# Attention and MLP on one core: dividing the eight PSUM banks 3 + 2 + 3 instead of 3 + 3 + 2

## The chip, the cores and the metric

The kernel runs on one core of a Trainium2 chip. Time is microseconds of device time for one execution. Three runs of the kernel before gave a median of 809.33 us (809.15 to 810.74). Besides these there is one execution taken by the profiler, from which every row and duration of the text comes.

## The reference

Two transformer layers over one sequence of 2048 rows of width 448, with the same weights in both. Each layer adds attention and then an MLP to its input:

```python
x = x + A(layernorm(x))      # A: softmax(q k^T * 28**-0.5) v, 16 heads of 28, then @ wo
x = x + B(layernorm(x))      # B: relu(h @ w1 + b1)**2 @ w2 + b2, 448 -> 1792 -> 448
x = x + A(layernorm(x))
x = x + B(layernorm(x))
```

Softmax needs one exponential for each of 2 x 16 x 2048 x 2048 scores. This is what fills the kernel's time.

## The kernel before, in words

**Units.** The scores are cut into 2048 units of 128 partitions x 512 columns of fp32, and one unit fills one PSUM bank. A unit belongs to a head, a few key blocks and a block of queries. The scores of a unit are K times Q (line 1106, four heads side by side in the rows of the array), then the exponential turns them into bf16 in SBUF (tile pts), then P times V (line 1335, into a bank called oT) uses them. A pass is all units of one layer, query block and group of four heads. The reference's maximum is not subtracted before the exponential, and the sum for the softmax comes out of P times V by a column of ones in V.

**Two ways to an exponential.** ScalarE does most units: one ACTIVATE with Exp (line 1138) over a whole score group, 1536 columns for three units (called wide in the text) or 1024 for two (narrow). The others go to VectorE and GpSimd, which work it out with integer tricks: VectorE reads the scores out of PSUM (line 1210), GpSimd makes a correction of it (1235, 1250), and VectorE squares and adds (1241, 1262, 1274). Such a unit is called VectorE's.

**PSUM.** The eight banks are two score tiles of three banks each (pool ps_sc, resource R_sc) and two spare banks (pools ps_m, resources R_m). While ScalarE reads one score tile, TensorE fills the other. The spare banks hold everything else that TensorE makes: the tiles of projections and of the MLP (mt, line 834), transposes (tp), P times V (oT). At the very beginning, and once the last scores are sent, these may also use score tiles (pools_now).

**Where VectorE's scores lie.** s_stream sends the score groups one after the other. It takes the next three units. Then either a fourth unit goes to VectorE in a spare bank (the branch with OWN3, `own`), or the group is cut to two units and the third bank of its tile gets a unit for VectorE (the branch with THIRD): ScalarE then reads two banks, VectorE the third, and the tile is free when both have read. The order has 373 wide and 298 narrow exponentials, and 333 units for VectorE: 298 in third banks and 35 in spare ones.

**What sets the order.** Planner.run is a list scheduler that runs when the kernel is built. Streams (scores, exponentials, P times V, projections, layer norm, fillers for TensorE) offer their next operation; the planner keeps a clock for each engine, and takes what can start earliest, by priority. So every engine's queue is fixed when the kernel is built, and on the chip each engine works through its queue in that order, waiting on semaphores. Tables of 128 numbers, one for each 16 units, steer it: OWN3 (may a fourth unit go to a spare bank here), PACE (how much VectorE may have waiting before it gets another unit), MIXT (whether GpSimd makes the second part of a unit). `apart` decides whether VectorE gets a unit at all. To keep TensorE's clock up, the planner repeats score matmuls while there is room (`again`) and adds fillers (`heat`, line 1766).

**Opening and tail.** The first exponential needs layer norm, transposes and the first K and Q of the first rows; layer norm's blocks for later rows are transposed by DMA (line 716). After the last exponential come P times V of the last rows, the normalisation, the output projection, layer norm, and the last rows' MLP (finish, ends_last).

Of the kernel before, what the change touches and what calls it, by code (L numbers as in the profile page):

```python
# [75 lines left out]
PRE = 0.5  # L76
# [22 lines left out]
OWN3 = (0.0, 0.0, 0.0, 0.0, 0.0, 0.0, 1.0, 1.0, 0.0, 0.0, 0.0, 0.0, 1.0, 0.0, 1.0, 1.0, 1.0, 1.0, 0.0, 1.0, 0.0, 0.0, 1.0, 0.0, 1.0, 1.0, 1.0, 0.0, 0.0, 0.0, 0.0, 1.0, 1.0, 1.0, 0.0, 0.0, 0.0, 1.0, 0.0, 1.0, 1.0, 0.0, 1.0, 0.0, 0.0, 0.0, 0.0, 0.0, 0.0, 1.0, 0.0, 0.0, 0.0, 0.0, 1.0, 0.0, 0.0, 0.0, 0.0, 0.0, 1.0, 1.0, 0.0, 0.0, 0.0, 1.0, 1.0, 0.0, 0.0, 0.0, 1.0, 0.0, 0.0, 1.0, 1.0, 0.0, 0.0, 1.0, 0.0, 0.0, 0.0, 0.0, 0.0, 0.0, 0.0, 0.0, 0.0, 0.0, 1.0, 0.0, 0.0, 1.0, 0.0, 1.0, 1.0, 0.0, 1.0, 1.0, 1.0, 1.0, 0.0, 0.0, 0.0, 0.0, 1.0, 0.0, 1.0, 1.0, 0.0, 1.0, 0.0, 0.0, 0.0, 0.0, 1.0, 1.0, 1.0, 0.0, 0.0, 0.0, 0.0, 0.0, 0.0, 0.0, 0.0, 0.0, 0.0, 0.0)  # L99
# [9 lines left out]
LEAD = 15  # L109
LAST = 690  # L110
BUSY = 0.995
PACE = (1.4, 3.0, 3.0, 1.4, 3.0, 1.4, 2.2, 4.0, 3.0, 3.4, 3.0, 3.0, 4.0, 2.2, 3.0, 3.0, 3.0, 3.4, 3.4, 3.4, 2.2, 2.2, 3.4, 3.0, 3.4, 4.0, 2.2, 3.0, 4.0, 3.0, 3.0, 4.0, 4.0, 3.4, 3.4, 4.0, 4.0, 3.4, 3.0, 4.0, 3.0, 4.0, 3.0, 4.0, 3.0, 3.0, 2.2, 3.0, 3.0, 3.4, 3.0, 3.0, 3.0, 3.0, 3.4, 4.0, 3.4, 4.0, 2.2, 4.0, 4.0, 4.0, 3.0, 2.2, 2.2, 2.2, 3.0, 3.0, 3.0, 3.0, 4.0, 4.0, 2.2, 4.0, 3.0, 4.0, 3.0, 3.4, 4.0, 3.0, 3.0, 1.4, 3.0, 3.4, 3.0, 4.0, 1.4, 3.4, 3.4, 4.0, 3.0, 2.2, 3.0, 3.0, 4.0, 3.4, 3.0, 4.0, 3.0, 2.2, 3.4, 2.2, 3.0, 3.4, 3.0, 4.0, 3.0, 3.0, 1.4, 4.0, 3.0, 3.0, 3.0, 2.2, 3.0, 2.2, 3.4, 3.0, 3.0, 3.0, 3.0, 3.0, 3.0, 3.0, 3.0, 3.0, 3.0, 3.0)
MIXT = (1.8, 1.2, 1.8, 1.2, 1.2, 1.8, -9.0, 1.2, 1.2, 1.8, 1.2, 1.2, 1.8, 1.2, 1.2, 1.8, 1.2, 1.2, -9.0, 1.2, 1.2, 1.2, 1.2, 1.2, -9.0, 1.8, 1.2, 1.2, 1.2, 1.2, -9.0, 1.2, 1.8, 1.2, 1.8, -9.0, 1.8, 1.2, 1.2, 1.2, 1.8, 1.2, 1.2, 1.2, 1.2, 1.2, 1.8, 1.2, 1.8, 1.2, 1.2, 1.2, 1.2, 1.2, -9.0, 1.8, 1.2, 1.8, 1.2, 1.2, 1.8, 1.2, -9.0, 1.2, -9.0, -9.0, 1.2, -9.0, 1.2, 1.8, 1.2, 1.8, -9.0, 1.2, 1.8, 1.8, 1.8, -9.0, 1.8, 1.2, 1.8, 1.2, 1.2, 1.8, 1.2, 1.2, 1.8, 1.2, 1.8, 1.8, -9.0, 1.2, -9.0, 1.8, 1.8, 1.2, 1.8, 1.2, 1.2, -9.0, -9.0, 1.2, 1.2, 1.2, 1.2, 1.2, -9.0, 1.2, -9.0, 1.2, 1.2, 1.2, -9.0, 1.2, -9.0, 1.2, 1.2, -9.0, 1.2, 1.2, 1.8, 1.8, 1.2, 1.2, 1.2, 1.2, 1.2, 1.2)
# [4 lines left out]
NPT = 12  # L118
# [4 lines left out]
LASTP = (3.2, 3.2, 3.2, 3.2, 3.2, 3.2, 3.2, 3.2, 3.2, 3.2, 3.2, 3.2, 3.2, 3.2, 3.2, 3.2, 3.2, 3.2, 3.2, 3.2, 3.2, 3.2, 3.2, 3.2, 3.2, 3.2, 3.2, 3.2, 3.2, 3.2, 3.2, 3.2, 3.2, 3.2, 3.2, 3.2, 3.2, 3.2, 3.2, 3.2, 3.2, 3.2, 3.2, 3.2, 3.2, 3.2, 3.2, 3.2, 3.2, 3.2, 3.2, 3.2, 3.2, 3.2, 3.2, 3.2, 3.2, 3.2, 3.2, 3.2, 3.2, 3.2, 3.2, 3.2, 3.2, 3.2, 3.2, 3.2, 3.2, 3.2, 3.2, 3.2, 3.2, 3.2, 3.2, 3.2, 3.2, 3.2, 3.2, 3.2, 3.2, 3.2, 3.2, 3.2, 3.2, 3.2, 3.2, 3.2, 3.2, 2.6, 3.2, 3.2, 3.2, 3.2, 3.2, 2.6, 1.5, 3.2, 2.6, 1.5, 3.2, 1.5, 3.2, 3.2, 3.2, 3.2, 1.5, 3.2, 4.4, 3.2, 3.2, 3.2, 3.2, 3.2, 3.2, 3.2, 3.2, 3.2, 3.2, 3.2, 3.2, 3.2, 3.2, 3.2, 3.2, 3.2, 3.2, 3.2)  # L123
# [15 lines left out]
LEND = 2  # L139
# [243 lines left out]
def kernel(  # L383
# [37 lines left out]
    ps_sc = ctx.enter_context(tc.tile_pool(name="ps_sc", bufs=2, space=bass.MemoryType.PSUM))  # L421
    ps_m = [ctx.enter_context(tc.tile_pool(name=f"ps_m{i}", bufs=1, space=bass.MemoryType.PSUM)) for i in range(2)]
# [4 lines left out]
    R_sc, R_m, R_pt = Res(2), (Res(1), Res(1)), Res(NPT)  # L427
# [612 lines left out]
    def s_stream():  # L1040
        while at[0] < len(units):
            gi = len(gbuf)
            js = ahead(3)
# [3 lines left out]
            def fn(e, gi=gi, us=us, js=js):  # L1047
                sc = ps_sc.tile([P, 3 * 512], DT.float32, name="sc", tag="sc")
# [10 lines left out]
                if OWN3[step[0]] > 0 and bank_free(o.start) and next_at(js[-1] + 1):  # L1059
# [7 lines left out]
                else:  # L1067
# [5 lines left out]
                    gbuf[gi]["in"] = not own and units[j][0] == us[0][0]  # L1073
# [25 lines left out]
                for i in list(range(4)) * (again + 1):  # L1099
                    for k, (pi, kb, r, hh) in enumerate(us):  # L1100
                        if i >= r:
# [9 lines left out]
                                   deps=list({d for u in us for d in needs(u)}), acq=R_sc, mode="row", sets=("s", gi))  # L1111
# [706 lines left out]
```

## Time and profile before

| | |
|---|---|
| median of three runs | 809.33 us |
| the profiled execution | 808.23 us, span 806.4 us |
| busy: ScalarE | 787.9 us (98%) |
| busy: VectorE | 765.0 us (95%) |
| busy: TensorE matmul | 758.2 us (94%) |
| busy: GpSimd | 483.4 us (60%) |
| first exponential begins | 10.71 us |
| last exponential ends | 792.9 us |
| granted TensorE clock | 1.000 |

PE is TensorE, PEld its weight loads, DVE VectorE, ACT ScalarE, POOL GpSimd; xN is a number of instructions. In a row of instruction groups stand the line, the engine, the operation, output<-inputs by the program's names with their shapes, and the count; then busy microseconds together and the mean nanoseconds of one; then idle time of the engine just before them, and what ended most of it. In a row of the timeline stand the start, the length of an unbroken run, and in brackets the idle time before it with what ended it; the run is listed under the shape of its first instruction. A row of waits reads "who <- for whom: us in total, times, longest". Neighbouring ScalarE instructions overlap in the records, so the sum of their durations is more than their busy time.

### The profile page before, as it was taken

The page shows a single profiled execution, that of the slowest core. Times are in us where ns is not written, and L with a number is a line of the kernel's source. Part 1 is how long each engine was busy: PE and PEld are TensorE (multiplying, and loading weights), DVE is VectorE, ACT ScalarE, POOL GpSimd, SP SyncE. Part 2 cuts the span into 40 slices and gives each one's busy share as a digit, 9 for nine tenths or more (in the row PEclk, how much of TensorE's full clock was granted, in tenths as well). Part 3 has the DMA queues.
Part 4 walks back from the last instruction along what each step waited for, and adds up shares of the span by engine and source line. Part 5 has one row for each costly group of instructions (what it writes and reads, how often), then busy time and mean ns, then how long its engine had stood idle before and what let it go on. Part 6 is the DMA issues. An engine that isn't in the chain of part 4 may idle for free.

```text
span 806.4 us, 27435 instructions
## 1 busy us (share of the span) xinstructions
PE 758.2 (94%) x11275; PEld 389.2 (48%) x11275; DVE 765.0 (95%) x1705; ACT 787.9 (98%) x686; POOL 483.4 (60%) x750
## 2 busy tenths in 40 slices
PE   8999989999899998999999998989899999999998
PEld 5544544444544544444544544434354444445565
DVE  7999999999999999999999998999999999999965
ACT  8999999999999999999999999999999999999994
POOL 3264656777676666866566666675665666666310
PEclk9999999999999999999999999999999999999999
DMA  9210010111002011001000000011100101010100
GB/s 249 84 22 9 15 23 10 22 22 22 19 4 35 10 22 21 5 20 22 15 16 15 13 3 15 9 21 25 34 21 14 34 14 34 10 26 9 31 16 13
DMA packets 59566, 20.66 MB, mean 26 GB/s; under 512 B 45289, under 2 KB 58987, under 8 KB 59440
## 3 DMA queue, kind: packets, MB, share of 16 engines
q1 hardware_dynamic: 59440, 18.91, 10.4%
q8 instruction: 88, 1.44, 0.8%
q14 instruction: 38, 0.31, 0.1%
HBM read 10.28 MB, written 1.95 MB: 15 GB/s over the span
## 4 chain that ended last, share of the span: by engine, by line
PE 39%; ACT 25%; DVE 24%; issue 9%; DMA 2%; POOL 1%; ACTq 0%; DVEq 0%; POOLq 0%
ACT pts L1138 25%; PE mt L834 19%; PE sc L1106 11%; PE oT L1335 7%; DVE v_w L1210 5%; DVE r L1531 3%; DVE pts L1262 2%; DMA xnT<-xn 2%; DVE pts L1241 2%; DVE st L661 2%; DVE K_sb L1210 1%; DVE x_sb L1473 1%; DVE V_sb L1241 1%; DVE V_sb L1540 1%; DVE V_sb L1262 1%
## 5 line engine op out<-in xcount | busy, mean ns | idle before, releaser
L1138 ACT ACTIVATE pts<-sc 128x1024 bf16<-128x1024 f32 (+1 forms) x671 | 777.8, 1321 | 5.0 <-PE sc L1106 4.2
L1106 PE MATMUL sc<-Q_sb,K_sb 32*128 32x256 bf16 (+1 forms) x4414 | 275.6, 265 | 31.2 <-ACT pts L1138 27.5
L1106 PEld LDWEIGHTS <-K_sb 32*128 32x128 bf16 x4484 | 102.8, 92 | 205.9 <-issue 145.6
L1250 POOL TENSOR_SCALAR v_w<-v_w 128x512 int16<-128x512 f32 x229 | 151.7, 662 | 65.9 <-DVE pts L1262 15.0
L1335 PE MATMUL oT<-pts,V_sb 128*32 128x256 bf16 (+1 forms) x4000 | 153.9, 268 | 0.8 <-DVE pts L1262 0.2
L1210 DVE TENSOR_SCALAR v_w<-sc 128x512 f32<-128x512 f32 x218 | 147.8, 681 | 2.9 <-PE sc L1106 2.1
L834 PE MATMUL mt<-xnT,w 128*128 128x256 bf16 (+1 forms) x888 | 119.4, 271 | 4.2 <-DVE r L1531 2.8
L1235 POOL TENSOR_SCALAR pts<-v_w 128x512 bf16<-128x512 uint16 x123 | 86.4, 703 | 53.2 <-DVE v_w L1210 15.6
L1335 PEld LDWEIGHTS <-V_sb 128*32 128x32 bf16 x4352 | 89.9, 96 | 51.2 <-issue 41.7
L1235 POOL TENSOR_SCALAR V_sb<-v_w 128x512 bf16<-128x512 uint16 x99 | 68.1, 688 | 47.5 <-DVE v_w L1210 11.5
L834 PEld LDWEIGHTS <-w 128*128 128x128 bf16 x896 | 75.2, 97 | 39.8 <-issue 30.6
L1250 POOL TENSOR_SCALAR K_sb<-K_sb 128x512 int16<-128x512 f32 x92 | 61.3, 666 | 32.2 <-DVE V_sb L1262 3.8
L1531 DVE TENSOR_SCALAR r<-mt 128x512 bf16<-128x512 f32 x108 | 73.8, 683 | 4.1 <-PE mt L834 1.9
L834 PE MATMUL mt<-w,V_sb 128*128 128x448 bf16 (+2 forms) x288 | 68.2, 346 | 0.0
L1241 DVE TENSOR_TENSOR pts<-pts 128x512 bf16<-128x512 bf16 (+1 forms) x124 | 64.7, 522 | 0.5 <-POOL pts L1235 0.5
L1210 DVE TENSOR_SCALAR K_sb<-sc 128x512 f32<-128x512 f32 x80 | 54.5, 682 | 5.5 <-PE sc L1106 4.7
L1241 DVE TENSOR_TENSOR V_sb<-V_sb 128x512 bf16<-128x512 bf16 (+1 forms) x106 | 56.4, 532 | 0.3 <-POOL V_sb L1235 0.3
L1262 DVE TENSOR_TENSOR pts<-pts,v_w 128x512 int16<-128x512 bf16 (+1 forms) x106 | 47.9, 452 | 0.9 <-POOL v_w L1250 0.5
L1473 DVE TENSOR_TENSOR x_sb<-x_sb,mt 128x448 bf16<-128x448 bf16 x61 | 37.2, 611 | 4.2 <-PE mt L834 3.9
L1235 POOL TENSOR_SCALAR V_sb<-K_sb 128x512 bf16<-128x512 uint16 x39 | 28.7, 736 | 20.6 <-DVE K_sb L1210 6.2
L1235 POOL TENSOR_SCALAR pts<-K_sb 128x512 bf16<-128x512 uint16 x43 | 29.6, 689 | 16.4 <-DVE V_sb L1262 3.5
L661 DVE BATCH_NORM_STATS2 st<-x_sb 128x6 f32<-128x448 bf16 x63 | 38.6, 615 | 0.9 <-DMA x_sb<-in_A_x_dram 0.7
(149 smaller groups left out, 854.1 us busy)
## 6 DMA issues: line engine op xcount, KB each, us to landing
rec<-scr SPq DMA_DIRECT2D x54, 64.0 KB
x_sb<-in_A_x_dram SPq DMA_DIRECT2D x8, 224.0 KB
out_dram<-x_sb SPq DMA_DIRECT2D x15, 112.0 KB
w<-in_B_w_dram SPq DMA_DIRECT2D x1, 1568.0 KB
w<-in_B_w_dram SPq DMA_DIRECT2D x1, 1344.0 KB
dn<-oT_sb SPq DMA_DIRECT2D x54, 2.0 KB
xnT<-xn SPq DMA_TRANSPOSE x50
V_sb<-in_A_wqkv_dram SPq DMA_DIRECT2D x4, 168.0 KB
```

The source lines that it names most:

```text
L661: return nc.vector.bn_stats(out=box["st"][:, :], in_=x_sb[:, t0 + j, :] if src is None else src())
L834: nc.tensor.matmul(box["t"][:, c0:c0 + n], lhsT=lhsT() if callable(lhsT) else lhsT, rhs=rhs, start=a, stop=b)
L1106: nc.tensor.matmul(dst[k][:, i * nt * P:(i + 1) * nt * P], lhsT=K_sb[l][rows, g, (kb + i) * P:(kb + i + 1) * P], rhs=Q_sb[rows, g, t0 * P: ...
L1138: t = nc.scalar.activation(out=pt[:, 0:n], in_=gbuf[gi]["sc"][:, 0:n], func=AF.Exp, scale=float(np.log(2.0)) * 2.0 ** -FRAC)
L1210: t = nc.vector.tensor_scalar(out=box["w"], in0=two(src), scalar1=EXP_SHIFT, scalar2=EXP_LOW, op0=ALU.add, op1=ALU.max)
L1235: return nc.gpsimd.tensor_scalar(out=two(pd), in0=low, scalar1=-EXP_MID * 65536, scalar2=EXP_BEND, op0=ALU.add, op1=ALU.mult)
L1241: return nc.vector.tensor_tensor(out=pd, in0=pd, in1=pd, op=ALU.mult)
L1250: return nc.gpsimd.tensor_scalar(out=two(box["t"]), in0=box["w"], scalar1=EXP_BITS, scalar2=1.0, op0=ALU.add, op1=ALU.mult)
L1262: return nc.vector.tensor_tensor(out=pd.bitcast(DT.int16), in0=pd, in1=t, op=ALU.add)
L1335: nc.tensor.matmul(box["t"][DHP * hh:DHP * hh + DHP, 0:n], lhsT=V_sb[l][:, kb + i, 4 * g + hh, :], rhs=p[:, c0:c0 + n], start=begin and kb ...
L1473: return nc.vector.tensor_tensor(out=x_sb[:, tb, lo:hi], in0=x_sb[:, tb, lo:hi], in1=t[:, 0:hi - lo], op=ALU.add)
L1531: return nc.vector.tensor_scalar(out=r[:, 0:w], in0=t[:, 0:w], scalar1=0.0, scalar2=None, op0=ALU.max)
```

## The change

- PSUM is divided anew: a score tile of three banks, one of two (`WIDE = (3, 2)`, pools ps_sc0 and ps_sc1), and three spare banks instead of two. The groups use the tiles in turn, so ScalarE reads three banks, two, three, two.
- VectorE's units no longer take the third bank of a group (`THIRD = 0`). They are all sent along with a group into a spare bank: with a narrow group wherever `apart` allows it, with a wide one where OWN3 allows it as well. What VectorE makes of a unit sent along with a narrow group may go into that group's free third of its pts slot (`gbuf[gi]["in"]`).
- Each score tile is a resource of its own: group gi waits for tile gi % 2, and nothing but ScalarE's exponential frees it.
- P times V and long matmul tiles that used to wait until both spare banks were free wait until two of the three are (`OPEN_M`).
- The tables OWN3 (107 ones, 44 before), PACE and MIXT are set anew; LASTP, STOPS and CPRE become constants, and LAST = 9999 no longer limits anything.

```diff
-LAST = 690
+LAST = 9999
...
-THIRD = 1
+THIRD = 0
+WIDE = (3, 2)
+OPEN_M = 2
+MMB = 3
+UNB = 0
...
-    ps_sc = ctx.enter_context(tc.tile_pool(name="ps_sc", bufs=2, space=bass.MemoryType.PSUM))
-    ps_m = [ctx.enter_context(tc.tile_pool(name=f"ps_m{i}", bufs=1, space=bass.MemoryType.PSUM)) for i in range(2)]
+    ps_sc = [ctx.enter_context(tc.tile_pool(name=f"ps_sc{i}", bufs=1, space=bass.MemoryType.PSUM)) for i in range(2)]
+    ps_m = [ctx.enter_context(tc.tile_pool(name=f"ps_m{i}", bufs=1, space=bass.MemoryType.PSUM)) for i in range(8 - sum(WIDE))]
...
-    R_sc, R_m, R_pt = Res(2), (Res(1), Res(1)), Res(NPT)
+    R_sc, R_m, R_pt = (Res(1), Res(1)), tuple(Res(1) for _ in ps_m), Res(NPT)
...
+    def scores(i):
+        return ps_sc[i].tile([P, WIDE[i] * 512], DT.float32, name="sc", tag="sc")
...
-                return R_m if all(r.when() is not None for r in R_m) else ()
+                return R_m[:MMB] if sum(r.when() is not None for r in R_m[:MMB]) >= OPEN_M else ()
...
-        if len(units) - i < STOPS[step[0]] or not LEAD <= len(gbuf) <= LAST:
+        if len(units) - i < STOP or not LEAD <= len(gbuf) <= LAST:
...
-            js = ahead(3)
+            js = ahead(WIDE[gi % 2])
...
-                sc = ps_sc.tile([P, 3 * 512], DT.float32, name="sc", tag="sc")
+                sc = scores(gi % 2)
...
-                if OWN3[step[0]] > 0 and bank_free(o.start) and next_at(js[-1] + 1):
+                if (OWN3[step[0]] > 0 or len(us) < 3) and bank_free(o.start) and next_at(js[-1] + 1):
                     j = apart(at[0], o.start, us)
                 elif len(us) == 3 and THIRD:
...
-                    gbuf[gi]["in"] = not own and units[j][0] == us[0][0]
+                    gbuf[gi]["in"] = len(us) < 4 and units[j][0] == us[0][0]
...
-                                   deps=list({d for u in us for d in needs(u)}), acq=R_sc, mode="row", sets=("s", gi))
+                                   deps=list({d for u in us for d in needs(u)}), acq=R_sc[gi % 2], mode="row", sets=("s", gi))
```

The change adds lines, so line 1106 of before is 1112 now, 1138 is 1144, 834 is 840 and 1210 is 1216.

How it moves instructions is seen in the built order of each engine's queue. First ScalarE's queue from the first Q tile on; pts is the output of the exponential, sc a score tile, and "x14" means 14 such instructions in a row. Before:

```order
L851 ACTIVATE Q_sb<-sc 128x2x256
L1138 ACTIVATE pts<-sc 128x1536 x14
L1138 ACTIVATE pts<-sc 128x1024 x2
L1138 ACTIVATE pts<-sc 128x1536 x6
L1138 ACTIVATE pts<-sc 128x1024 x4
L1138 ACTIVATE pts<-sc 128x1536 x3
```

And the same place now, with the numbers of the tiles:

```order
L857 ACTIVATE Q_sb_107<-mt_232 128x2x256
L1144 ACTIVATE pts_119<-sc_266 128x1536
L1144 ACTIVATE pts_119<-sc_273 128x1024
L1144 ACTIVATE pts_119<-sc_294 128x1536
L1144 ACTIVATE pts_119<-sc_322 128x1024
L1144 ACTIVATE pts_119<-sc_331 128x1536
```

Wide and narrow ones now take turns from the first group to the last, also where VectorE takes no units; before, narrow ones stood only where VectorE had the third bank. Over the whole program there are 346 wide and 347 narrow ones now, 693 in place of 671, and 316 units for VectorE in place of 333, all of them in spare banks.

Second, TensorE's queue ahead of the first scores; xnT is the transposed layer norm of the first rows, wk and wq are weights, sc_254 and sc_266 are the first score tiles. Of several matmuls that read alike one is shown. Before:

```order
L834 MATMUL sc_226<-xnT_168,wq_90 128x256
L834 LDWEIGHTS wk_91
L834 MATMUL mt_239<-xnT_168,wk_91 128x256
L1106 LDWEIGHTS K_sb0_99
L1106 MATMUL sc_254<-Q_sb_101,K_sb0_99 128x256
```

And now:

```order
L840 MATMUL mt_232<-xnT_174,wq_96 128x256
L840 LDWEIGHTS wk_97
L840 MATMUL mt_244<-xnT_174,wk_97 128x256
L840 LDWEIGHTS wq_96
L840 MATMUL mt_260<-xnT_174,wq_96 128x256
L1112 LDWEIGHTS K_sb0_105
L1112 MATMUL sc_266<-Q_sb_107,K_sb0_105 128x256
```

Four matmuls of the second Q tile (mt_260), which stood behind the first two score groups, stand ahead of the first one now; the first Q tile (mt_232) lies in a spare bank where it lay in a score tile.

More of the change, by code (lines that the diff above doesn't have):

```diff
@@ L1078, in fn @@
                         x = gbuf[gi]["x"] = Op("PE", 0.0, None)
-                        x.res = min((r for r in R_m if r.when() is not None), key=lambda r: r.when())
+                        x.res = (lambda f: f[-1] if UNB else min(f, key=lambda r: r.when()))([r for r in R_m if r.when() is not None and (not UNB or r.when() <= o.start)])
                         x.turn = len(x.res.rel)
```

17 lines of the change are left out of this document (8 added, 9 removed).

## The prediction

> **What bounds the kernel now.** I read the page's busy times first, then the busy time by stretch, then ScalarE's own timeline, and last the two shapes of its exponential.
>
> ```profile
> PE 758.2 (94%) x11275; PEld 389.2 (48%) x11275; DVE 765.0 (95%) x1705; ACT 787.9 (98%) x686; POOL 483.4 (60%) x750
> core 0: us, PE busy (x) PEld busy (x) DVE busy (x) ACT busy (x) POOL busy (x), PEclk, DMA share, GB/s
> 0.00:10.70 10.70, 9.32 (x65) 5.49 (x65) 7.04 (x29) 7.68 (x10) 4.77 (x13) 1.00 0.79 211
> 10.70:792.90 782.20, 738.46 (x11091) 376.27 (x11088) 750.54 (x1651) 777.76 (x671) 478.05 (x736) 1.00 0.10 23
> 792.90:806.40 13.50, 10.39 (x124) 7.44 (x122) 7.46 (x26) 2.49 (x6) 0.56 (x1) 1.00 0.06 19
> ```
>
> Three engines look full, but only one is. Between 10.7 and 792.9 us ScalarE does nothing but its 671 exponentials, and is busy for 777.76 of 782.20 us; VectorE and TensorE have 32 and 44 us to spare there. So the time is an opening of 10.7 us, a chain of exponentials, and a tail of 13.5 us. ScalarE's timeline shows where that chain breaks:
>
> ```profile
> 10.71 6.82 ACT L1138 ACTIVATE pts<-sc 128x1536 bf16<-128x1536 f32 x5 [0.61 <-PE sc L1106]
> 18.00 81.82 ACT L1138 ACTIVATE pts<-sc 128x1536 bf16<-128x1536 f32 x70 [0.46 <-PE sc L1106]
> 100.06 40.93 ACT L1138 ACTIVATE pts<-sc 128x1536 bf16<-128x1536 f32 x34 [0.24 <-PE sc L1106]
> 141.24 89.23 ACT L1138 ACTIVATE pts<-sc 128x1024 bf16<-128x1024 f32 x78 [0.25 <-PE sc L1106]
> 230.75 57.49 ACT L1138 ACTIVATE pts<-sc 128x1536 bf16<-128x1536 f32 x50 [0.28 <-PE sc L1106]
> 288.49 33.19 ACT L1138 ACTIVATE pts<-sc 128x1536 bf16<-128x1536 f32 x29 [0.24 <-PE sc L1106]
> 322.27 1.02 ACT L1138 ACTIVATE pts<-sc 128x1024 bf16<-128x1024 f32 x1 [0.59 <-PE sc L1106]
> 323.45 156.53 ACT L1138 ACTIVATE pts<-sc 128x1536 bf16<-128x1536 f32 x136 [0.16 <-PE sc L1106]
> 480.19 18.35 ACT L1138 ACTIVATE pts<-sc 128x1536 bf16<-128x1536 f32 x16 [0.22 <-ACT pts L1138]
> 499.93 292.99 ACT L1138 ACTIVATE pts<-sc 128x1024 bf16<-128x1024 f32 x252 [1.38 <-PE sc L1106]
> ```
>
> A row is one unbroken run (the shape printed is that of its first instruction); the bracket is the idle time ahead of it. Inside the chain there are nine, 3.8 us together (what else is idle lies in gaps too short for a row of their own), each a score group that TensorE delivered late. Whatever the change does, it has to show in this chain, in its ends, or not at all.
>
> **The change part by part.**
>
> *ScalarE's work.* The price of one exponential comes from these rows: the two shapes, the first instruction alone, and a run of 21 wide ones.
>
> ```profile
> L1138 ACT ACTIVATE pts<-sc 128x1536 bf16<-128x1536 f32 x373 | 533.7, 1511 | 2.4 <-PE sc L1106 2.0 <-ACT pts L1138 0.2
> L1138 ACT ACTIVATE pts<-sc 128x1024 bf16<-128x1024 f32 x298 | 305.8, 1083 | 2.6 <-PE sc L1106 2.2
> 10.71 1.45 ACT L1138 ACTIVATE pts<-sc 128x1536 bf16<-128x1536 f32 x1 [0.61 <-PE sc L1106]
> 764.61 28.32 ACT L1138 ACTIVATE pts<-sc 128x1536 bf16<-128x1536 f32 x21
> ```
>
> Neighbours overlap, so the cost is the step from one to the next: (28.32 - 1.45) / 20 = 1.3435 us for a wide one. The mean durations differ by 1511 - 1083 = 428 ns, the price of one more bank, so a narrow one costs 0.9155 us, and 1.3435 - 3 x 0.428 = 0.06 us of each is fixed. Before: 373 x 1.3435 + 298 x 0.9155 = 773.9 us. So 782.2 - 773.9 = 8.3 us of the chain is lost: 4.4 us idle (782.20 - 777.76), and 3.9 us in instructions that began late and overlapped less.
>
> The order of the changed kernel has 346 wide and 347 narrow exponentials. 373 x 3 + 298 x 2 = 1715 units before, 346 x 3 + 347 x 2 = 1732 now; of 2048 units VectorE keeps 316 where it had 333. ScalarE gets 17 units x 0.428 = 7.3 us and 22 instructions x 0.06 = 1.3 us: **+8.6 us**, all on the path. The chain without any loss is then 782.6 us, as long as the chain of before with all its losses. That is the core of this forecast: the change can at best give back what it takes.
>
> [...]
>
> *The losses.* What can the change give back? Two gaps are TensorE standing in its queue before a transposed block that a DMA brings, with the next scores behind it:
>
> ```profile
> 320.81 1.03 PE L834 MATMUL mt<-xnT,wk 128*128 128x256 bf16 x8 [0.94 <-DMA xnT<-xn]
> 498.90 0.60 PE L834 MATMUL mt<-xnT,wk 128*128 128x256 bf16 x4 [1.45 <-DMA xnT<-xn]
> 139.89 0.92 PE L834 MATMUL mt<-wo,oTn 128*128 128x448 bf16 x4 [0.23 <-DVE oT_sb L1362]
> 287.50 0.36 PE L834 MATMUL mt<-w,K_sb 128*128 128x448 bf16 x1 [0.20 <-DVE K_sb L1210]
> PE sc L1106 <- ACT pts L1138: 27.5, 61, 0.9
> PEld L1106 <- DVE v_w L1210: 10.6, 35, 0.8
> ```
>
> They cost ScalarE 0.59 + 0.16 + 1.38 = 2.1 us, and a PSUM bank more doesn't make a DMA land sooner: they stay, perhaps at other places. The 0.46 us at 18.00, in the opening, stays too: 2.6 of the 4.4 us. The rest, 1.8 us, are gaps of a quarter of a microsecond behind rows like the one at 139.89 and at 287.50 (TensorE held until VectorE has emptied a bank), and behind the 35 fills whose first weight load waited 10.6 us in total for VectorE to read its third of the old group. The third spare bank, and score tiles that only ScalarE reads, take these away: I count them gone. The 3.9 us of late starts I split in the same ratio (2.6 to 1.8): 1.6 us go. **-3.4 us**; 4.9 us of loss stay. The ends: all 8.3 us go, or none, and then 22 more groups at 8.3 / 671 = 0.012 us lose 0.3 us besides.
>
> *The opening.* Before, TensorE goes from the K matmuls straight to the first scores. In the new order four of the next tile's Q matmuls stand between.
>
> ```profile
> 8.43 1.04 PE L834 MATMUL sc<-xnT,wq 128*128 128x256 bf16 x8
> 9.30 1.04 PE L834 MATMUL mt<-xnT,wk 128*128 128x256 bf16 x8
> 9.51 0.60 ACT L851 ACTIVATE Q_sb<-sc 128x512 bf16<-128x512 f32 x1 [1.21 <-PE sc L834]
> 10.28 0.61 PE L1106 MATMUL sc<-Q_sb,K_sb 32*128 32x256 bf16 x12
> L834 PE MATMUL mt<-xnT,wq 128*128 128x256 bf16 x184 | 25.2, 274 | 0.0
> ```
>
> Eight such matmuls take 1.04 us, one 0.274: a step is (1.04 - 0.274) / 7 = 0.109 us and four are 0.44 us. Q is ready at 10.11 and the scores start at 10.28, as soon as the K matmuls have left, so only about 0.1 us could hide: **+0.4 us** for the first exponential (0.2 to 0.6), and the whole chain moves with it.
>
> *The tail.* The same matmuls in nearly the same order behind the last exponential: 0, within 0.5 us either way, since five places for tiles replace four.
>
> *TensorE and VectorE.* The new order has 100 more repeated score matmuls and 7 more fillers. By the page's row below that is 100 x 275.6 / 4414 = 6.2 us, and 7 x 0.355 = 2.5 us.
>
> ```profile
> L1106 PE MATMUL sc<-Q_sb,K_sb 32*128 32x256 bf16 (+1 forms) x4414 | 275.6, 265 | 31.2 <-ACT pts L1138 27.5
> L1766 PE MATMUL mt<-xn,ident 128*128 128x448 bf16 x89 | 26.0, 355 | 0.4 <-DVE oT_sb L1362 0.3
> L1210 DVE TENSOR_SCALAR v_w<-sc 128x512 f32<-128x512 f32 x218 | 147.8, 681 | 2.9 <-PE sc L1106 2.1
> L1106 PE MATMUL mt<-Q_sb,K_sb 32*128 32x256 bf16 x70 | 13.8, 272 | 0.0
> ```
>
> The 27.5 us in which TensorE waits for ScalarE hide these 8.7 us; without that cover they would all be added. VectorE loses 17 units, at least 17 x 0.681 = 11.6 us of its 750.54; it isn't what ends the chain, so that gains nothing by itself.
>
> *The sum.* 8.6 - 3.4 + 0.4 = **+5.6 us**. The profiled execution took 808.23 us with a span of 806.4, so one like it would take 813.8. It lies 1.1 us below the median of the runs, 809.33, to which I add the same 5.6: **814.9 us**.
>
> **The rivals.** What a measurement of this kernel can tell from no change is about 0.2%, 1.6 us. With L us of loss left, the sum is 0.7 + L (8.6 - 8.3 + 0.4 + L).
>
> *Not slower.* Every loss goes, because TensorE, with a third bank for its own tiles, runs far enough ahead to cover late DMAs as well. It decides at L = 0.9: below that the time is within 0.2%, with L = 0.4 it is 810.4. For it: nine gaps are few, and VectorE has more air. Against it: 2.1 us of the idle time is a DMA's, and TensorE stands in one queue. 0.10.
>
> *Faster.* In the old kernel VectorE reads the third bank of the very tile that ScalarE reads, and if this slowed ScalarE, tiles of its own would speed it up. But that could only be part of the 3.9 us, which are already in the 8.3; a gain of 1.6 us would need 2.3 us more out of a tail of 13.5. The time would be 807.5. 0.04. [...]
>
> *Refills come late.* Now every second exponential is narrow, and in its 0.9155 us TensorE has to refill the three banks just read. If one in eight of the 347 windows is missed by 0.25 us (the gaps at 100.06 to 288.49), that is 43 x 0.25 = 10.8 us more: 825.7; half as many give 820.3. For it: TensorE waits for ScalarE only 61 times in 671 groups, so mostly it is the later one. Against it: 298 windows were as narrow before, and the idle time is the same ahead of both shapes (2.4 and 2.6 us). 0.12.
>
> *Banks run short.* 316 units now sit in spare banks instead of 35 (the 70 matmuls into mt). Each holds a bank for its fill and read, at most the 0.61 us of the double fill at 10.28 and 0.68 us: 316 x 1.29 = 408 us, where the third bank brings 782. So this should be relief; if it went wrong, so that the 3.4 us that I count gone came back half as large again, that is 5.1 us more: 820.0. 0.08.
>
> **How the numbers follow.** The forecast has 0.66, and its own bounds are L of 1 to 8.6: 811.0 to 818.6. The range reaches down to 810.4 for half of the first rival, and up to 820.5 for the shortage of banks and the milder late refills; left out are the faster case, half of "not slower" and the worse refills, 0.15, and what lies beyond the forecast's own bounds. Slower: 0.66 + 0.12 + 0.08 = 0.86; within 0.2%: 0.10; faster: 0.04.
>
> **What would show it.** Right: 346 and 347 exponentials of unchanged step; a chain of 784 to 791 us (782.6 + 4.9 = 787.5 by the sum); the first one at about 11.1 us; gaps behind xnT still there, those behind VectorE's reads gone, and almost no fill waiting for line 1210's read. Wrong: a chain of 783 us or less with hardly a gap (the first rival), wide exponentials with steps below 1.34 us (the second), many gaps of a quarter of a microsecond ahead of wide exponentials (late refills), or TensorE waiting for spare banks.

## The result, and the profile after

| | before | after |
|---|---|---|
| median of four runs each | 809.4 us (809.15 to 810.74) | 821.78 us (820.13 to 823.69) |
| profiled execution | 808.23 us, span 806.4 | 820.13 us, span 818.3 |

After is slower: ratio 1.0152, 95% interval 1.0132 to 1.0172. The direction is the one forecast; the size, +12.4 us in the medians where +5.6 was forecast, lies outside the range.

The busy times and the same three stretches of the page after, with the columns PE, PEld, DVE, ACT and POOL busy, granted clock, DMA share and GB/s:

```profile
PE 772.6 (94%) x11378; PEld 399.1 (49%) x11378; DVE 759.3 (93%) x1693; ACT 796.7 (97%) x708; POOL 447.7 (55%) x701
0.00:11.10 11.10, 9.72 (x66) 5.91 (x67) 7.40 (x29) 7.61 (x10) 4.78 (x13) 1.00 0.79 218
11.10:805.00 793.90, 752.61 (x11201) 385.78 (x11199) 744.46 (x1639) 786.62 (x693) 442.35 (x687) 1.00 0.10 23
805.00:818.30 13.30, 10.24 (x124) 7.36 (x124) 7.47 (x26) 2.48 (x5) 0.56 (x1) 1.00 0.06 18
```

ScalarE is still what fills the middle. Its timeline, one row for each unbroken run of exponentials, the idle time ahead of it in brackets:

```profile
11.20 6.88 ACT L1144 ACTIVATE pts<-sc 128x1536 bf16<-128x1536 f32 x6 [1.05 <-PE sc L1112]
18.27 169.72 ACT L1144 ACTIVATE pts<-sc 128x1536 bf16<-128x1536 f32 x149 [0.19 <-PE sc L1112]
188.46 65.99 ACT L1144 ACTIVATE pts<-sc 128x1024 bf16<-128x1024 f32 x58 [0.47 <-PE mt L1112]
255.31 21.37 ACT L1144 ACTIVATE pts<-sc 128x1024 bf16<-128x1024 f32 x19 [0.86 <-PE mt L1112]
277.20 17.27 ACT L1144 ACTIVATE pts<-sc 128x1536 bf16<-128x1536 f32 x15 [0.52 <-PE mt L1112]
295.40 55.57 ACT L1144 ACTIVATE pts<-sc 128x1024 bf16<-128x1024 f32 x49 [0.93 <-PE sc L1112]
352.07 347.47 ACT L1144 ACTIVATE pts<-sc 128x1536 bf16<-128x1536 f32 x306 [1.10 <-PE mt L1112]
699.73 66.05 ACT L1144 ACTIVATE pts<-sc 128x1536 bf16<-128x1536 f32 x58 [0.20 <-PE mt L1112]
767.42 37.42 ACT L1144 ACTIVATE pts<-sc 128x1536 bf16<-128x1536 f32 x33 [1.63 <-PE mt L1112]
```

The first exponential begins at 11.20 (10.71 before), the last ends at 767.42 + 37.42 = 804.84, and 13.5 us of tail follow, as before. So the chain is 793.6 us. Its 346 wide and 347 narrow exponentials cost 782.5 us by the forecast's prices; the rest of the chain, 11.1 us, is called the loss, and before it was 8.3. The span grew by 11.9 us: 8.6 of ScalarE's work, 2.8 of loss, 0.5 of opening.

Four of the gaps are TensorE standing in front of a block that a DMA transposes, and two (188.46 and 277.20) are TensorE waiting until VectorE has read a score out of a spare bank. TensorE's rows for these, and its waits in total (waiting for whom: us, times, longest):

```profile
253.84 1.05 PE L840 MATMUL mt<-xnT,wk 128*128 128x256 bf16 x8 [1.05 <-DMA xnT<-xn]
293.75 1.03 PE L840 MATMUL mt<-xnT,w 128*128 128x256 bf16 x8 [1.09 <-DMA xnT<-xn]
351.04 0.60 PE L840 MATMUL mt<-xnT,wk 128*128 128x256 bf16 x4 [1.15 <-DMA xnT<-xn]
766.38 0.60 PE L840 MATMUL mt<-xnT,w 128*128 128x256 bf16 x4 [2.01 <-DMA xnT<-xn]
187.11 0.36 PE L840 MATMUL mt<-w,K_sb 128*128 128x448 bf16 x1 [0.68 <-DVE K_sb L1216]
PE mt L840 <- DMA xnT<-xn: 5.5, 5, 2.0
PE mt L840 <- DVE v_w L1216: 1.6, 7, 0.3
PE mt L840 <- DVE K_sb L1216: 1.0, 2, 0.7
```

Before, the row of its waits behind the DMA was:

```profile
PE mt L834 <- DMA xnT<-xn: 3.1, 4, 1.4
```

Behind the DMA are 0.86 + 0.93 + 1.10 + 1.63 = 4.5 us of ScalarE's idle time, where it was 2.1. The weight loads' waits for VectorE's read of a third bank (10.6 us, 35 times before) have no row left, as forecast. But waits for VectorE's read (line 1216) are not gone: they moved from the score tiles to the spare banks.

### The profile page after: what moved, and what is told of

Its sections match the earlier page's. It is cut to its first block, busy times and chain, and to the rows that moved or that the text cites. A ratio compares the mean times of both kernels' runs of the same rounds, so it can differ in the third digit from the quotient of the medians.

```text
span 818.3 us, 27502 instructions
## 1 busy us (share of the span) xinstructions
PE 772.6 (94%) x11378; PEld 399.1 (49%) x11378; DVE 759.3 (93%) x1693; ACT 796.7 (97%) x708; POOL 447.7 (55%) x701
## 4 chain that ended last, share of the span: by engine, by line
ACT 40%; PE 37%; issue 11%; DVE 9%; DMA 3%; POOL 1%; ACTq 0%; DVEq 0%; POOLq 0%
ACT pts L1144 40%; PE mt L840 16%; PE sc L1112 11%; PE oT L1341 6%; DMA xnT<-xn 2%; DVE v_w L1216 2%; PE mt L1772 1%; DVE V_sb L1268 1%; DVE K_sb L1216 1%; DVE Q_sb L859 1%; DVE pts L1268 1%; DVE V_sb L1247 1%; PE mt L1112 1%; DVE pts L1247 1%; DVE r L1537 1%
## 5 line engine op out<-in xcount | busy, mean ns | idle before, releaser
L1144 ACT ACTIVATE pts<-sc 128x1536 bf16<-128x1536 f32 (+1 forms) x693 | 786.6, 1290 | 8.1 <-PE mt L1112 4.8
L1112 PE MATMUL sc<-Q_sb,K_sb 32*128 32x256 bf16 (+1 forms) x3868 | 286.7, 265 | 31.4 <-ACT pts L1144 28.4
L1112 PEld LDWEIGHTS <-K_sb 32*128 32x128 bf16 x4584 | 114.0, 92 | 210.6 <-issue 204.2
L1256 POOL TENSOR_SCALAR v_w<-v_w 128x512 int16<-128x512 f32 x204 | 136.5, 669 | 68.2 <-DVE pts L1268 12.5
L1216 DVE TENSOR_SCALAR v_w<-mt 128x512 f32<-128x512 f32 x227 | 154.8, 683 | 11.0 <-PE mt L1112 9.7
L1112 PE MATMUL mt<-Q_sb,K_sb 32*128 32x256 bf16 (+1 forms) x716 | 131.2, 268 | 0.1
L1241 POOL TENSOR_SCALAR pts<-v_w 128x512 bf16<-128x512 uint16 x95 | 66.3, 698 | 54.5 <-DVE v_w L1216 23.0
L1216 DVE TENSOR_SCALAR K_sb<-mt 128x512 f32<-128x512 f32 x89 | 60.8, 684 | 3.3 <-PE mt L1112 2.5
L1268 DVE TENSOR_TENSOR V_sb<-V_sb,v_w 128x512 int16<-128x512 bf16 (+1 forms) x95 | 42.9, 452 | 2.4 <-POOL v_w L1256 1.0
L1341 PE MATMUL oT<-V_sb,V_sb 128*32 128x256 bf16 (+1 forms) x296 | 40.4, 274 | 0.1
```

The lines of the kernel that those rows point to most:

```text
L1112: nc.tensor.matmul(dst[k][:, i * nt * P:(i + 1) * nt * P], lhsT=K_sb[l][rows, g, (kb + i) * P:(kb + i + 1) * P], rhs=Q_sb[rows, g, t0 * P: ...
L1144: t = nc.scalar.activation(out=pt[:, 0:n], in_=gbuf[gi]["sc"][:, 0:n], func=AF.Exp, scale=float(np.log(2.0)) * 2.0 ** -FRAC)
L1216: t = nc.vector.tensor_scalar(out=box["w"], in0=two(src), scalar1=EXP_SHIFT, scalar2=EXP_LOW, op0=ALU.add, op1=ALU.max)
L1241: return nc.gpsimd.tensor_scalar(out=two(pd), in0=low, scalar1=-EXP_MID * 65536, scalar2=EXP_BEND, op0=ALU.add, op1=ALU.mult)
L1256: return nc.gpsimd.tensor_scalar(out=two(box["t"]), in0=box["w"], scalar1=EXP_BITS, scalar2=1.0, op0=ALU.add, op1=ALU.mult)
L1268: return nc.vector.tensor_tensor(out=pd.bitcast(DT.int16), in0=pd, in1=t, op=ALU.add)
```

## The experiments

The theory after the result (A): the work term is right, and the loss grew because TensorE's waits for transposed blocks doubled, while the freed waits for VectorE were worth little. The rivals: the new bank division makes the refills late by itself, or the spare banks are short, or the tables alone do it.

**Taking the DMA waits out.** In after and in before, matmuls that would read a DMA-transposed block read the fixed tile wk, which has the same layout. The DMAs still run, and every queue keeps its order.

```diff
+        by_dma = []
...
+                by_dma.append(1)
...
+        still = wk[:, :, :, :].rearrange("p c h r -> p c (h r)")[:, :, 0:QR]
-        return xnT, own_xt, ends
+        return still if by_dma else xnT, own_xt, ends
```

> The changed kernel, in the same order, but the matmuls that read a block transposed by DMA read a fixed tile (wk) instead, so that nobody waits for those transposes; they are still made and take the same time. The values of Q, K, V and of the MLP are then not those of the reference. Theory A (late transposes are the largest part of the loss that stayed): the four gaps of 0.86, 0.93, 1.10 and 1.63 us go, and with each about 0.1 us of late start, so 4.9 us: from 821.8 to about 817, a chain of exponentials of 788.7 us instead of 793.6. Rival B (the refill behind a narrow exponential is late, and the DMA only happens to be what TensorE stands behind): the gaps come back under another name, 820 to 822. Rival C (spare banks run short): the same as B, with TensorE waiting for VectorE's evacuations.

> The kernel before with the same edit as e1. Theory A: the gaps of 0.59, 0.16 and 1.38 us go, 2.4 us with their late starts: 807.0. The distance between e1 and e2 is then about 10 us (8.6 of ScalarE's work, 0.5 of the opening, the rest other losses) where it is 12.4 with the waits. Rivals B and C: 809, no change.

Measured: 814.94 us for after (814.9 to 815.22; ratio to before 1.0071, interval 1.0056 to 1.0086) and 805.8 us for before (805.55 to 806.05; ratio 0.9956, 0.9940 to 0.9973). Chain and ScalarE's two shapes in after with the fixed tile:

```profile
11.20:799.60 788.40, 752.42 (x11189) 386.54 (x11187) 743.79 (x1639) 785.94 (x693) 440.79 (x687) 1.00 0.10 23
L1147 ACT ACTIVATE pts<-sc 128x1536 bf16<-128x1536 f32 x346 | 522.6, 1510 | 2.2 <-PE sc L1115 1.2 <-PE mt L1115 0.7
L1147 ACT ACTIVATE pts<-sc 128x1024 bf16<-128x1024 f32 x347 | 375.3, 1082 | 1.3 <-PE mt L1115 0.5
PE mt L843 <- DVE v_w L1219: 1.9, 8, 0.3
PE mt L843 <- DVE K_sb L1219: 1.0, 2, 0.7
```

The chain is 788.4 us where 788.7 was expected, a loss of 5.9. The time fell 2 us further than expected because the expectation started from the median; against after's profiled execution, 820.13, it fell by 5.2. The same stretch in before with the fixed tile:

```profile
10.90:790.60 779.70, 738.73 (x11095) 377.02 (x11088) 750.59 (x1651) 777.41 (x671) 477.97 (x736) 1.00 0.11 23
```

Its first exponential begins at 10.98, so the chain is 779.6 and the loss 779.6 - 773.9 = 5.7. Two things follow. The DMA waits cost before 8.3 - 5.7 = 2.6 us and after 11.1 - 5.9 = 5.2. And without them both kernels lose the same: the medians differ by 9.1 us, almost all of it ScalarE's 8.6. The rival of late refills falls too: behind 347 narrow windows the wide exponentials wait 2.2 us in all, 1.05 of them ahead of the very first.

The four runs of after with the fixed tile lie within 0.32 us of each other, those of after within 3.56; their granted clocks are compared below.

**Only the tables, only the branch.** After with the three tables of before, and before with VectorE's units sent to the two spare banks:

```diff
-OWN3 = (1.0, 1.0, ...)
+OWN3 = (0.0, 0.0, ...)
...
-PACE = (3.0, 3.0, ...)
-MIXT = (1.8, 1.2, ...)
+PACE = (1.4, 3.0, ...)
+MIXT = (1.8, 1.2, ...)
```

```diff
-OWN3 = (0.0, 0.0, ...)
+OWN3 = (1.0,) * 128
...
-THIRD = 1
+THIRD = 0
```

> The changed kernel with the tables OWN3, PACE and MIXT of before. Its order gives VectorE 275 units, ScalarE 355 wide, 354 narrow and one of 512 columns. Theory A (time is the opening, 1.3435 us a wide and 0.9155 us a narrow exponential, a loss, and the tail): 801.0 + 11.2 + 13.5 + 1.8 and a loss of 8 to 13 us, 835 to 841. Rival B (late refills behind narrow ones bound it): with 354 narrow instead of 347, 822 to 824.

> The kernel before, 3 + 3 + 2, but VectorE's scores in spare banks only (THIRD = 0, OWN3 all ones). The order gives VectorE 192 units, ScalarE 618 wide ones. Theory A: 831.2 us of exponentials, 10.7 + 13.5 + 1.8 us around them and a loss of 5 to 10 us: 862 to 867. Rival (VectorE, 95% busy, is as much the bound as ScalarE): with 141 units less VectorE has 200 us to spare, and the time falls or stays within 809 to 830.

Measured: 846.99 us (844.33 to 852.11; ratio 1.0473, 1.0434 to 1.0513) and 874.58 us (872.44 to 877.24; ratio 1.0808, 1.0783 to 1.0834). First after with the old tables, then before with spare banks alone: the wide shape and the row that names the wait.

```profile
L1144 ACT ACTIVATE pts<-sc 128x1536 bf16<-128x1536 f32 x355 | 534.2, 1505 | 6.1 <-PE sc L1112 4.1 <-PE oT L1341 1.6
```

```profile
L1138 ACT ACTIVATE pts<-sc 128x1536 bf16<-128x1536 f32 x618 | 835.0, 1522 | 10.5 <-PE sc L1106 4.6 <-PE mt L1106 4.6 <-ACT pts L1138 0.2
```

With the old tables VectorE gets 274 units (the trace has 274 of its reads; the expectation says 275) and ScalarE's work without loss is 801.5 us, so the tables are worth 801.5 - 782.5 = 19.0 us of it. With two spare banks and no third banks VectorE gets 192 units (618 wide exponentials, one narrow): 831.2 us. In that plan two spare banks hold far fewer than the 316 that three hold in after. Both times are above what was expected: the chains are 820.6 and 845.8 us, so 19.1 and 14.6 us are lost.

**Reckoning with slower transposes.** A pair of DMA transposes, and the matmul that waits for it, in after: 766.38 - 760.50 = 5.9 us, and in the first gap of the four 253.84 - 248.32 = 5.5 us.

```profile
248.32 2.54 SPq L722 DMA_TRANSPOSE xnT<-xn  x2
760.50 2.55 SPq L722 DMA_TRANSPOSE xnT<-xn  x2
```

The planner reckons 3.7 us (2 x 1.3 + 2.0 - 0.9). TensorE came to these two blocks 3.9 and 4.5 us after the issue (its waits of 2.01 and 1.05 us taken off), so the issue was not late by the plan: the transposes took longer than it reckons. Three kernels give it more: after everywhere, before in one stretch, after behind unit 1800.

```diff
-TLAT = -0.9
+TLAT = 1.1
```

```diff
-            o = Op("DMA", TURN * len(xs), by, deps=[x[1] for x in xs], lat=TLAT)
+            o = Op("DMA", TURN * len(xs), by, deps=[x[1] for x in xs], lat=0.1 if 1150 <= at[0] < 1400 else TLAT)
```

```diff
-            o = Op("DMA", TURN * len(xs), by, deps=[x[1] for x in xs], lat=TLAT)
+            o = Op("DMA", TURN * len(xs), by, deps=[x[1] for x in xs], lat=1.1 if at[0] >= 1800 else TLAT)
```

> The kernel after with one number of the planner changed: it reckons 2 us more from a DMA transpose to its landing (TLAT 1.1 in place of -0.9), 5.7 us for a pair, about what a pair took in the trace of after (5.3 to 5.9). Everything is computed. The plan comes out anew: 298 units for VectorE in place of 316, so ScalarE's exponentials without loss are 790.6 us in place of 782.5. Theory A (the DMA waits come from a plan that puts the consuming matmul too early): TensorE's waits for xnT fall below 1 us, the loss of the chain falls from 11.1 to about 6 us as in the runs with the fixed tile, span 11.2 + 790.6 + 6 + 13.5 = 821.3, time about 823 with a small spread. Theory B (TensorE meets late transposes wherever they are planned): waits for xnT stay at 3 us or more, loss about 11 us, time 828.

> The kernel before with 1 us more reckoned for a DMA transpose, only while the scores go from unit 1150 to 1400, where the gap of 1.38 us was (at 499.9 us of its trace). Everything is computed; up to there the order is that of before. VectorE has 332 units in place of 333, ScalarE 774.3 us without loss in place of 773.9. Theory A (the wait for the transposed block was the gap): the gap shrinks by 1 us or more, so span 806.4 + 0.4 - 1.2 = 805.6, time about 808.6, ratio 0.999; a small gain that may lie within the spread. Theory B (the gap only moves to another block): span 806.8 or more, ratio 1.000 to 1.002.

> The kernel after with 2 us more reckoned for a DMA transpose, only from unit 1800 on, where the largest gap was (1.63 us at 767.4). Everything is computed. ScalarE's queue is word for word that of after, 316 units and 782.5 us without loss; TensorE's differs from there on only. Theory A: the gap at 767 goes, the others stay: chain 793.6 - 1.6 = 792.0, span 816.7, time about 1.6 us below after's, 820 for the median. Theory B: another wait takes its place, chain 793 or more.

Measured: 848.14 us (847.27 to 849.07; ratio 1.0493, 1.0475 to 1.0510), 817.64 us (816.84 to 819.53; ratio 1.0115, 1.0098 to 1.0132) and 819.4 us (818.09 to 821.11; ratio 1.0135, 1.0115 to 1.0154). The first two missed by far. ScalarE's timeline in after with slow transposes everywhere, then in before with the one stretch, at their largest gaps:

```profile
588.74 4.62 ACT L1144 ACTIVATE pts<-sc 128x1024 bf16<-128x1024 f32 x4 [4.15 <-PE oT L1341]
776.02 11.45 ACT L1144 ACTIVATE pts<-sc 128x1536 bf16<-128x1536 f32 x10 [7.04 <-PE oT L1341]
```

```profile
500.01 60.60 ACT L1138 ACTIVATE pts<-sc 128x1536 bf16<-128x1536 f32 x53 [0.21 <-ACT pts L1138]
564.30 37.29 ACT L1138 ACTIVATE pts<-sc 128x1536 bf16<-128x1536 f32 x32 [3.69 <-PE oT L1335]
```

What was aimed at did go: in the first, TensorE has no row of waits for xnT any more; in the second, the gap of 1.38 us at 499.93 is 0.21 at 500.01. But everything that the planner ordered afterwards is new, and in the new orders the exponential waits up to 7 us for P times V, which holds the slots of pts that it writes to. The chains are 818.9 and 790.8 us, 27.7 and 15.9 of them lost (791.1 and 774.8 without loss). That the tables fit only the order that they were set for is the likely reason; no run here tests it. Whether the plan of after could be spared its DMA waits at a profit stays open; these runs don't show it.

The third kernel keeps ScalarE's queue word for word. Its timeline from 255 us on:

```profile
255.26 21.37 ACT L1144 ACTIVATE pts<-sc 128x1024 bf16<-128x1024 f32 x19 [0.79 <-PE mt L1112]
277.15 17.27 ACT L1144 ACTIVATE pts<-sc 128x1536 bf16<-128x1536 f32 x15 [0.52 <-PE mt L1112]
296.75 1.02 ACT L1144 ACTIVATE pts<-sc 128x1024 bf16<-128x1024 f32 x1 [2.33 <-PE sc L1112]
298.05 54.71 ACT L1144 ACTIVATE pts<-sc 128x1536 bf16<-128x1536 f32 x48 [0.27 <-PE sc L1112]
354.08 347.45 ACT L1144 ACTIVATE pts<-sc 128x1536 bf16<-128x1536 f32 x306 [1.33 <-PE mt L1112]
701.73 103.30 ACT L1144 ACTIVATE pts<-sc 128x1536 bf16<-128x1536 f32 x91 [0.20 <-PE mt L1112]
```

The gap at 767 is gone: the run that begins at 701.73 goes on to the last exponential. Its two runs at a granted clock of 1.000 took 818.09 and 818.41 us, after's one such run 820.13: 1.7 to 2.0 us for a gap of 1.63. Yet this profiled execution is no shorter: its chain of 793.8 us is the number of theory B, but no other wait took that gap's place. What grew lies ahead of the edit: at 296 us, where the order is still that of after, 2.33 + 0.27 us were idle in place of 0.93. Three stretches there, TensorE's busy time being the first number behind the comma and the granted clock the third from the end, first in this kernel:

```profile
292.00:294.00 2.00, 0.42 (x7) 0.16 (x7) 1.82 (x6) 2.00 (x3) 0.75 (x2) 1.00 0.33 6
294.00:296.00 2.00, 2.00 (x9) 1.09 (x9) 0.23 (x1) 0.42 (x1) 0.79 (x2) 0.53 0.02 1
296.00:298.00 2.00, 2.00 (x22) 0.81 (x25) 2.00 (x6) 1.02 (x1) 0.83 (x2) 0.61 0.00 0
```

And in after:

```profile
292.00:294.00 2.00, 0.65 (x9) 0.37 (x9) 1.87 (x6) 2.00 (x3) 0.70 (x2) 1.00 0.06 2
294.00:296.00 2.00, 2.00 (x23) 1.09 (x20) 1.18 (x3) 1.07 (x2) 0.92 (x3) 1.00 0.00 0
296.00:298.00 2.00, 2.00 (x51) 1.24 (x48) 1.53 (x5) 2.00 (x3) 1.28 (x2) 1.00 0.07 2
```

In both TensorE stands idle for most of 292 to 294 us, waiting for the block above all. In the one the clock is 0.53 and 0.61 for the next 4 us, in the other 1.00. So in this execution a wait for a transposed block cost its own length, and a stretch at about half clock followed. That the wait brings it on isn't shown by this one trace alone, but the mean clocks fit: the four kernels that keep the order of before or after and wait for no such block (the two above, and two with short reads below) had 1.000 in all of their 16 executions. After's runs at mean clocks of 0.996 to 0.998 took 821.36 to 823.69 us; before's runs beside all these kernels had a median of 810.11 us at 0.997 to 0.998 (nine runs) and of 808.71 at 1.000 (19 runs).

**What VectorE's reads cost.** Without DMA waits, does VectorE cause the rest of the loss? One run takes its units away; two shorten its reads of the units that go into v_w, 227 of 316 in after and 239 of 333 in before.

```diff
-                if (OWN3[step[0]] > 0 or len(us) < 3) and bank_free(o.start) and next_at(js[-1] + 1):
+                if len(us) < 0 and bank_free(o.start) and next_at(js[-1] + 1):
```

```diff
+        nc.gpsimd.memset(v_w[:], 0.0)
...
-            t = nc.vector.tensor_scalar(out=box["w"], in0=two(src), scalar1=EXP_SHIFT,
+            n = 32 if k < 4 else 256
+            t = nc.vector.tensor_scalar(out=box["w"][:, :, 0:n], in0=two(src)[:, :, 0:n], scalar1=EXP_SHIFT,
```

> The kernel after with the fixed tile in place of the DMA-transposed blocks (as in the first run), and VectorE gets no units at all: 410 wide and 409 narrow exponentials, 925.3 us without loss. Values of projections and MLP from those blocks are not the reference's. Theory A (the 5.9 us of loss that are left without DMA waits come from VectorE's units, which hold spare banks and keep TensorE and VectorE late): the loss falls to 2 us or less though there are 18% more exponentials, most of it in the opening; chain about 927, span about 952. Theory B (the loss comes with the turn of wide and narrow groups themselves, so many hundredths per group): the loss stays at 6 to 7 us, span about 956.

> The first run's kernel (after, fixed tile in place of the DMA-transposed blocks) in which VectorE reads only 64 of the 512 columns of a spare-bank score, for the units that it puts into v_w (about two in three); the other columns keep older values, so those exponentials are not the reference's. The order of every engine is that of after but for one memset. VectorE's read falls from 0.68 to an estimated 0.2 us, so spare banks come free earlier and VectorE runs up to 100 us below its 759. Theory A (of the 5.9 us of loss left without DMA waits, only what TensorE waits for VectorE is due to banks; the rest is TensorE's own work ahead of the next scores, which no bank changes): the two gaps at 188.4 and 276.3 shrink (1.0 us of idle time), TensorE's waits for line 1216's read fall from 3.2 us to under 1.5, and the loss falls to 4.2 to 5.2 us; time 814. Theory B (VectorE's units in spare banks cause most of it): the loss falls to 2.5 us or less, time 811.5.

> The same edit in before with the fixed tile: VectorE reads 64 columns of the third bank in place of 512 for the units that go to v_w. TensorE's waits ahead of score groups for VectorE's read of the third bank (PEld, 10.6 us, 35) should nearly vanish, and VectorE has 100 us more air. Theory A (those waits cost next to nothing, since ScalarE's own part of the tile ends later): the loss goes from 5.7 to 4.5 us or more, time within 1.2 us of the 805.8 of the second run. Theory B (my forecast's step: sharing the tile with VectorE is what costs the 1.8 us of short gaps and 1.6 us of late starts): the loss falls by 3 us or more, to under 2.7, time 802.8 or less.

The first took 965.83 us (span 964.0) and answered nothing: the chain ran from 11.19 to 948.54, a loss of 12.1 us, more than either theory, and its gaps of 0.44 to 1.55 us stand between 324 and 333 us and between 386 and 395, where the clock was down: 0.74 from 325 to 340 us and 0.69 from 385 to 400, with 1.00 from 400 to 560.

```profile
385.00:400.00 15.00, 15.00 (x166) 7.54 (x166) 3.65 (x7) 11.61 (x11) 0.00 (x0) 0.69 0.09 18
845.29 103.25 ACT L1147 ACTIVATE pts<-sc 128x1536 bf16<-128x1536 f32 x91 [0.17 <-PE oT L1344]
```

The short reads took 814.65 us (814.64 to 814.76; ratio 1.0059, 1.0039 to 1.0080) in after and 804.75 us (804.73 to 804.85; ratio 0.9937, 0.9920 to 0.9954) in before. The added memset delays their first exponential to 12.31 and 11.91, so the chains are compared. After:

```profile
12.30:799.30 787.00, 751.97 (x11189) 386.30 (x11187) 673.78 (x1639) 785.18 (x693) 445.13 (x687) 1.00 0.11 23
PE mt L844 <- DVE K_sb L1221: 0.6, 2, 0.3
276.37 419.61 ACT L1148 ACTIVATE pts<-sc 128x1536 bf16<-128x1536 f32 x370 [0.52 <-PE mt L1116]
```

And before:

```profile
11.90:789.50 777.60, 738.16 (x11091) 376.94 (x11088) 681.78 (x1651) 776.31 (x671) 486.64 (x736) 1.00 0.11 23
PEld L1110 <- DVE v_w L1215: 11.6, 45, 0.4
```

After loses 787.0 - 782.5 = 4.5 us, as theory A had it, though of the two gaps only the one at 188 went (276.37 is left, VectorE's read there being one that was not shortened). Before loses 777.6 - 773.9 = 3.7, between the two theories. So VectorE, its shortened reads and the 70 us less work together, is behind 1.4 us of after's loss and 2.0 of before's; what the reads cost that were not shortened stays open. And the waits of the weight loads for the third bank, which were to vanish, are still there, 11.6 us in 45 places beside a loss of 3.7 from all causes: on average at most a third of such a wait reaches ScalarE.

**Two banks for the tiles, and TensorE without its repeats.**

```diff
-MMB = 3
+MMB = 2
```

```diff
-                for i in list(range(4)) * (again + 1):
+                for i in range(4):
...
-                    for _ in range(k):
-                        nc.tensor.matmul(t[:, 0:D], lhsT=ident[:, :], rhs=xns[0][:, 0:D], start=True, stop=True)
+                    for _ in range(1):
+                        nc.tensor.matmul(t[:, 0:32], lhsT=ident[:, :], rhs=xns[0][:, 0:32], start=True, stop=True)
```

> The first run's kernel (after with the fixed tile), but projections, MLP and P times V may use only two of the three spare banks, as before the change; the third takes only VectorE's units. The plan comes out anew: 310 units for VectorE, 785.2 us of exponentials without loss, 2.7 more. Theory A (a third bank for TensorE's tiles buys almost nothing, TensorE is not short of banks for them): loss 5 to 8 us, span 816 to 819. Theory B (the third bank is what keeps the tiles from waiting): TensorE waits for VectorE's copies out of banks (lines 1368, 1537 and the like, under 1 us in the first run) for 5 us or more and the loss is over 10 us, span over 821. A new plan alone has cost gaps of several us behind P times V, which would show as gaps of ScalarE behind oT and are then taken out.

> The kernel of the ninth run (after, fixed tile, VectorE's short reads), without the work that TensorE does only to keep its clock up: score matmuls are not repeated, and a filler is one matmul of 32 columns in place of one or two of 448. The planner still reckons with them, so the order is the same but for these rows. Theory A (the 4.5 us of loss left in the ninth run are TensorE's own work ahead of the next scores, the repeats and fillers among it): late exponentials fall from 27 to 15 or fewer, the loss to 3 us or less, and the clock stays at 1.000. Theory B (the repeats and fillers keep the clock up, and without them it dips): a granted clock below 0.99 and a loss of 8 us or more. Theory C: loss 4 to 5 us, clock 1.000: neither counts, the lateness is of the needed work.

The first took 837.62 us (one run, span 835.8), with a loss of 20.4, much of it at single places of a new order. It is inconclusive:

```profile
520.66 2.37 ACT L1147 ACTIVATE pts<-sc 128x1024 bf16<-128x1024 f32 x2 [6.58 <-PE mt L1115]
PE sc L1115 <- DVE K_sb L866: 5.3, 3, 4.8
```

The second took 836.01 us (831.89 to 838.05; ratio 1.0315, 1.0284 to 1.0346), where the ninth took 814.65, with a loss of 810.4 - 782.5 = 27.9 us and a clock of 0.943 over the whole span in its profiled execution: theory B. Where it was down:

```profile
540.00:600.00 60.00, 52.84 (x650) 24.36 (x649) 45.75 (x121) 54.25 (x48) 34.10 (x52) 0.72 0.11 22
```

The repeats and fillers earn their place: without them the kernel takes 21.4 us more, at mean clocks of 0.943 to 0.957 where all four runs of the ninth had 1.000. Whether the last 4.5 us are TensorE's needed work ahead of the next scores, these runs can't tell.

## Why the prediction was right in direction and wrong in size

- *ScalarE's work*, +8.6 us: right. With the DMA waits out of both kernels the medians differ by 9.1 us, the losses by 0.2 and the openings by 0.2. The core of the forecast, that the change can at best give back what it takes, held.
- *The losses*, -3.4 us: this step failed; +2.8 was measured. It failed twice. Of the 2.1 us behind xnT it said "they stay, perhaps at other places". They moved, and doubled: 4.5 us of gaps, 5.2 of loss where there had been 2.6. The matmuls of the new order come to their blocks before these have landed four times at the cost of 0.86 to 1.63 us, against three gaps before. Why the new order has more such places is not shown; the planner reckons the same 3.7 us in both. And of the 1.8 us of short gaps and 1.6 of late starts it said "I count them gone": with the DMA waits out, 5.7 us before and 5.9 after, nothing had gone. The waits that it built on, 10.6 us ahead of score groups, did vanish, without the loss getting smaller. Waits behind VectorE took their place in the spare banks (1.4 us of loss where 2.0 were, as far as the shortened reads show it), and what is lost with VectorE so relieved is 4.5 where it was 3.7; of these 0.8 the cause stays open. In sum 2.6 - 0.6 + 0.8 = 2.8.
- *The opening*, +0.4: right, 0.49, from 10.71 to 11.20. *The tail*, 0: right, 13.5 both times.
- *TensorE and VectorE*: hidden, as forecast, in the sense that no longer busy time shows in the chain by itself (TensorE 752.61 us busy in it, 738.46 before); a part of the 0.8 may be theirs.
- From profiled execution to median: the forecast carried +5.6 over, and the median gained +12.4 where the profiled one gained 11.9; the profiled execution of after is the one with a clock of 1.000, the other three are at 0.996 to 0.998.
- The rivals: "not slower" and "faster" are out, with a step of the exponentials that didn't change (the 8 wide and 7 narrow ones from 277.20 on took 17.27 us; by the prices, with 1.45 for the first, 17.26). "Late refills" is out (2.2 us of idle time ahead of wide exponentials without the DMA). "Banks run short" named the right place, tiles held until VectorE reads a spare bank, at 1.4 us; it was not what set the size. That waits for transposed blocks double had no rival of its own.
- Small slips, which change neither the sum nor a chance: the chain without loss is 782.5 us, not 782.6; the gain of 1.6 us in the rival "faster" gives 807.7 us, not 807.5; and of the nine gaps the one at 480.19 is behind the exponential before it, not behind a late score group.

No kernel here that computes the whole result beats both. Before with the DMA waits out, which reads a fixed tile in place of the blocks, shows with 805.8 us what a plan that hides the waits could gain: about 4 us, if the rest of the order stayed.

## What to carry to other kernels

A wait counts only if the engine that sets the end waits because of it: look for it behind that engine's gaps before counting it gone. Here 10.6 us of the weight loads' waits vanished, and the loss grew by 2.8 us. Where a planner fixes the order, a change of resources can move the waits for a transfer, as it did those for the transposed blocks (3.1 us in 4 places before, 5.5 in 5 after); give such waits a term with ends on both sides, and not "they stay". Compare two such kernels with the suspected wait out of both: the orders stay as they are, where a changed number of the planner brought, in two of three kernels here, a new one with losses of its own.

## What was unexpected of the hardware

- From its issue to the matmul that waits for it, a pair of 128x512 transposes by DMA took 5.3 to 5.9 us in after, where the planner reckons 3.7. The queue was held for 2.52 to 2.55 us of this by the two, about 1.27 us each, and the matmul began only 2.8 to 3.3 us after that.
- One order of instructions met a clock of 0.53 and 0.61 for 4 us in one execution (the third kernel with slower transposes, from 294 us) and 1.00 in another (after). In the 2 us ahead TensorE was busy for 0.42 us in the first and for 0.65 in the second. What decides between the two is not shown.
- VectorE's read of 64 columns out of PSUM took 0.22 us (in after with the fixed tile and short reads, the row below) where 512 took 0.68 (in after).

```profile
L1221 DVE TENSOR_SCALAR v_w<-mt 128x64 f32<-128x64 f32 x227 | 49.9, 220 | 23.6 <-PE mt L1116 20.9 <-PE sc L1116 0.5
```
